# Tile 0's softmax sums on GpSimd in an attention and feed-forward kernel on one core, with the order of all work dealt anew

## The chip, the cores and the metric

One core of a Trainium2 chip (trn2) runs the whole kernel; the other cores are idle. The metric is device time in microseconds for one launch, from the kernel's own start to its end. The kernel before was timed three times: 800.82, 801.04 and 800.82 us.

## The reference

Linear attention whose output goes through one feed-forward block. `q`, `k` and `v` have the shape (8, 8, 576, 64): 8 batches, 8 heads, 576 positions, 64 features.

```python
def _attn_ref(q, k, v):
   q_s = q - np.max(q, axis=-1, keepdims=True)
   q_s = np.exp(q_s)
   q_s = q_s / (np.sum(q_s, axis=-1, keepdims=True) + 1e-09)
   k_s = k - np.max(k, axis=2, keepdims=True)
   k_s = np.exp(k_s)
   k_s = k_s / (np.sum(k_s, axis=2, keepdims=True) + 1e-09)
   kv = np.einsum('bhsd,bhse->bhde', k_s, v)
   return np.einsum('bhsd,bhde->bhse', q_s, kv).astype(np.float32)

def _moe_ref(x, w_in, w_out):        # x: 4608 x 512, w_in: 512 x 2048, w_out: 2048 x 512
    h = x @ w_in
    g = np.maximum(h, 0.0) + np.log1p(np.exp(-np.abs(h)))   # softplus
    return (g @ w_out).astype(np.float32)
```

Between the two, the heads are put side by side: x is 4608 tokens by 512.

## The kernel before, in words

The 4608 tokens are nine tiles of 512 (`TOK`). Tile 0 is worked alone; tiles 1 to 8 are worked in four pairs, whose two matrix products are done by seven block products instead of eight. Float32 products are made of rounded halves (`fp32r`, a high and a low part, three matmuls); only in tile 0 a few products use whole float32 (slower, but no split is needed first): the x of tile 0 (`x_first`) and the first two of its 16 blocks of the hidden layer.

All engines take their work in the order of one long list, `ORDER`, of some 2200 tokens. Each token calls one small function, which issues one to a few instructions on the engine that the function names. There is no scheduler at run time: an engine takes its own instructions strictly in the order of the list, and waits at one whose input is not ready. A second list, `HOMES`, says which slot of on-chip memory each buffer takes; a load into a slot waits until its last reader is done.

Tokens that matter here (tile 0, batch 0):

- `b0`, `b1`: load the two halves of tile 0's q (0.5 MB each). `n`: load the next k and v block (`kv_load`: two small fills of unused rows, the main load from SyncE, the tail's load from ScalarE's queue for the first four). `l3`: load the raw weights of block 3.
- `q0.0`, `q0.1` (`top`): maxima of the two halves of q. `q0.2` (`join`): joins maxima between the two partition groups that share a token's head; four ScalarE copies (`swapped`) and one VectorE maximum. `q0.3`, `q0.4` (`shift`): subtract the maxima; `q0.5`, `q0.6` (`power`): exp on ScalarE; `q0.7`, `q0.8` (`total`): sums of exp, a reduction on VectorE; `q0.12`, `q0.13` (`swap`): a TensorE matmul that joins the sums; `q0.9` (`invert`): their reciprocals; `q0.10`, `q0.11` (`divide`). A trailing `.1` on a q token puts it on GpSimd: before, these are `q0.4.1` and `q0.11.1`.
- `k0.h.i`, for the heads' pair h = 0 to 3: `.1` transposes of k on TensorE, `.2` (`across`) its maxima, `.3` their spread on TensorE, `.4` the subtraction, `.5` exp on ScalarE, `.6` the kv products on TensorE, `.7` (`scale`) reciprocals, `.8` (`keep`) two ScalarE copies of the scaled kv.
- `x0.h.0` (`flip`) a VectorE transpose of q, `.1` its product with kv, `.2` (`take`) out of PSUM, `.3` and `.4` the high and low part of x.
- Weights of block j: `Tj`, `Mj`, `Sj`, `Jj` rebuild float32 words, `Pj` and `Qj` split them in two. ScalarE does T, M and P, VectorE J and Q, a few S and Q are on GpSimd.
- `B0` to `B3`: the first hidden block by whole float32, one matmul per head pair. `Uj`: hidden block j, `Aj`: its softplus on ScalarE, `Gj`: the split of the result, `Oj`: its product with the output weights. `U1` and `O0`, `O1` are whole float32 too.
- `wA.n`: n warm-up matmuls on the identity, whose results nobody reads. They stand where TensorE would be idle before the first products.

At the start `first`, one float per partition, is filled and added to itself on GpSimd (line 1073), before anything else is asked of that engine. Its result is read by nobody.

The list before begins as follows, and the head that matters ends at `U2`:

```
    w0.20 b0 b1 q0.0 n k0.0.1 n q0.1 n n q0.2 q0.3 q0.4.1 l0 q0.5 l1 k0.0.2 k0.1.1 l2 k0.1.2 k0.0.3 k0.2.1 k0.0.4
    k0.0.5 q0.6 k0.1.3 k0.2.2 w5.5 k0.2.3 k0.1.4 k0.2.4 k0.1.5 l3 q0.7 k0.3.1 k0.3.2 k0.0.6 k0.0.7 T0 M0.1 T1 k0.1.6
    q0.8 k0.3.3 q0.12 w1.6 q0.13 k0.2.5 k0.2.6 k0.3.4 k0.3.5 k0.3.6 n z0 M1.1 k0.0.8 q0.9 q0.10 w2.3 k0.1.7 w3.2
```

Of the kernel before, what the change touches and what calls it, by code (L numbers as in the profile page):

```python
# [7 lines left out]
F32 = mybir.dt.float32  # L8
F32R = mybir.dt.float32r
U8 = mybir.dt.uint8  # L10
# [49 lines left out]
    Q9 D9 k1.3.5 q1.8 k1.2.6 k1.2.7 q1.5 q1.7 k1.3.6 k1.3.7 P11 A8 U9 k1.2.8 k1.2.9 D8 q1.9 Q11 q1.10 U10 q1.11 T12 G8  # L60
    D2 D1 x1.0.0 W0 A9 T13 G9 A10 M13.1 U11 M14.1 x1.0.1 O8 M12.1 J13 O9 x1.0.2 k2.0.0 P0 x1.0.3 D11 J12 G10 k1.3.8
    k1.3.9 P12 x1.1.0 Q12 Q0 M15.1 O10 x1.1.1 x1.1.2 T14 U12 P13 Q13 J14 D12 A11 x1.0.4 x1.0.5 x1.1.3 x1.1.4 U13
    x1.2.0 G11 O11 x1.1.5 k2.1.0 k2.1.1 x1.2.1 x1.2.2 x1.2.3 D10 P14 Q14 k2.1.2 A12 T15 J15 x1.2.4 k2.1.3 k2.1.4
    x1.3.0 U14 D0 A13 G12 D4 G13 P15 x1.3.1 A14 O12 x1.2.5 k2.0.1 x1.3.2 x1.3.3 k2.0.2 Q15.1 k2.0.3 k2.1.5 L2 k2.0.4
    O13 k2.0.5 x1.3.4 x1.3.5 U15 G14 k2.0.6 k2.1.6 y1.8 y1.9 y0.11 y1.11 D3 O14 A15 y0.8 G15 O15 q2.0 q2.1 n q2.2
    k2.0.7 k2.0.8 k2.1.7 k2.1.8 U16 U17 k2.0.9 A16 U18 n q2.4.1 q2.6 k2.1.9 k2.2.0 k2.3.0 k2.3.1 A17 U19 q2.3 D15 y0.9
    y1.10 y1.0 A18 y1.1 q2.8 y1.2 D14 k2.2.1 y0.10 D13 L3 y1.3 U20 k2.2.2 k2.3.2 k2.3.3 q2.5 q2.7 k2.2.3 q2.9 k2.2.4
    A19 q2.10 U21 A20 U22 y1.4 R0.0 y1.5 y1.6 A21 U23 x2.0.0 x2.0.1 q2.11 x2.0.2 y2.10 k2.3.4 A22 x2.0.3 k2.2.5 U24
    x2.0.4 y1.7 y0.0 y0.1 x2.0.5 k2.3.5 k2.2.6 A23 q3.0 y2.8 k2.2.7 k2.2.8 k2.2.9 L4 A24 k2.3.6 k2.3.7 y3.8 k2.3.8 U25
    x2.2.0 n n q3.1 k2.3.9 x2.1.0 A25 R0.1 x2.1.1 y2.9 U26 A26 q3.12 U27 A27 y2.11 R4.1.1 x2.1.2 x2.1.3 x2.1.4 U28  # L70
    y0.2 R0.2 x2.2.1 R4.3.1 k3.0.0 U29 q3.2 R4.0.1 y3.10 y3.9 A28 y0.3 y0.4 k3.0.4 y3.11 q3.4 x2.2.2 A29 U30 y0.5
    k3.0.5 q3.6 x2.1.5 x2.3.0 q3.3 x2.2.3 x2.3.1 x2.3.2 x2.2.4 y2.0 x2.2.5 U31 x2.3.3 A30 y2.1 y2.2 x2.3.4 x2.3.5 y2.3
    y0.7 y0.6 k3.1.0 r0.1 e0.0.0.0 A31 F0.2 F0.1 R0.3 U32 A32 F0.0 U33 q4.0 q4.1 q3.5 k3.1.4 q3.7 U34 k3.1.5 k3.1.6
    k3.0.6 A33 U35 q3.8 q3.13 q3.9 A34 q3.10 q4.12 q4.2 k3.0.7 k3.1.7 n U36 y3.0 A35 k3.0.8 y3.1 U37 y3.2 R0.4 y3.3
# [1155 lines left out]
```

## Time and profile before

| what | us |
| --- | --- |
| median of three timed runs | 800.82 |
| the profiled execution, its own time | 800.14 |
| its span, first to last instruction | 798.4 |
| TensorE (PE) busy in the span | 789.0 |
| VectorE (DVE) busy | 643.8 |
| ScalarE (ACT) busy | 516.6 |
| GpSimd (POOL) busy | 130.3 |

The span is the time from the first instruction to the last in one profiled launch; 1.74 us of that launch lie outside it. Its own time is 0.68 us under the median of the timed runs. Busy times are unions of an engine's instructions. A matmul's end is modelled, so "busy" on PE means that the engine had a matmul under way, not that it ran at its peak. In the rows below a start is counted from the span's beginning.

### The profile page before, as it was taken

The numbers are of one execution on the slowest core, as the hardware profiler recorded it, in microseconds if no ns is written. First come the engines' busy times: TensorE is split into PE (matmuls) and PEld (weight loads), VectorE is DVE, ScalarE is ACT, GpSimd is POOL, SyncE is SP. The second block draws the span as 40 slices with busy tenths as digits, with TensorE's granted clock in tenths as the row PEclk, the third lists the DMA queues.
The fourth block names the chain that finished last, engine by engine and source line by source line (L and its number), as shares of the span: only waits on it lengthen the run. The fifth ranks groups of instructions, "written<-read, shape, count | busy, mean of one in ns | idle before, by whom it ended". The sixth has DMA issues, their size and how long they took to land.

```text
span 798.4 us, 11786 instructions
## 1 busy us (share of the span) xinstructions
PE 789.0 (99%) x4196; PEld 646.8 (81%) x4196; DVE 643.8 (81%) x869; ACT 516.6 (65%) x768; POOL 130.3 (16%) x249
## 2 busy tenths in 40 slices
...
GB/s 336 371 344 292 321 252 286 289 295 281 325 276 275 238 276 256 288 292 276 263 322 183 288 281 186 238 219 184 328 136 242 269 145 204 136 215 348 145 51 69
DMA packets 137402, 200.01 MB, mean 251 GB/s; under 512 B 9920, under 2 KB 106432, under 8 KB 132224
## 3 DMA queue, kind: packets, MB, share of 16 engines
...
q14 instruction: 25, 0.20, 0.1%
...
## 4 chain that ended last, share of the span: by engine, by line
PE 94%; DVE 2%; DMA 2%; POOL 1%; ACT 1%; issue 0%; POOLq 0%; SPq 0%; ACTq 0%; DVEq 0%
PE po L980 9%; PE po L981 9%; PE po L982 9%; PE po L872 6%; PE po L874 6%; PE po L873 6%; PE ph L752 5%; PE ph L754 5%; PE ph L753 5%; PE ph L980 4%; PE ph L981 4%; PE ph L982 4%; PE ph L872 3%; PE ph L874 3%; PE ph L873 3%; PE att L544 2%
## 5 line engine op out<-in xcount | busy, mean ns | idle before, releaser
L1026 POOL DMA_DIRECT2D out<-w x108 | 69.7, 652 | 139.9 <-DVE w L1018 136.1
L960 ACT CAST w<-w 128x1024 fp32r<-128x1024 f32 x53 | 55.6, 1052 | 35.0 <-PE po L981 26.5
L963 DVE TENSOR_TENSOR w<-w,w 128x1024 fp32r<-128x1024 f32 x53 | 64.4, 1219 | 12.1 <-ACT w L960 12.0
L980 PE MATMUL po<-w,w 128*128 128x512 f32 x160 | 62.8, 392 | 0.0
L981 PE MATMUL po<-w,w 128*128 128x512 f32 x160 | 62.3, 390 | 0.0
L982 PE MATMUL po<-w,w 128*128 128x512 f32 x160 | 62.3, 389 | 0.0
L944 DVE TENSOR_TENSOR w<-w,w 128x1024 f32<-128x1024 f32 x44 | 53.3, 1215 | 0.3
...
L960 ACT CAST gg<-w 128x1024 fp32r<-128x1024 f32 x33 | 34.7, 1051 | 17.8 <-PE po L981 10.6
L873 PE MATMUL po<-w,w 128*128 128x512 f32 x118 | 46.0, 390 | 0.0
L872 PE MATMUL po<-w,w 128*128 128x512 f32 x108 | 42.6, 394 | 0.0
L874 PE MATMUL po<-w,w 128*128 128x512 f32 x108 | 42.1, 389 | 0.0
L963 DVE TENSOR_TENSOR gg<-w,gg 128x1024 fp32r<-128x1024 f32 x33 | 40.1, 1216 | 1.7 <-ACT gg L960 1.7
L493 DVE TENSOR_REDUCE mx<-kvt 128x128 f32<-128x640 f32 x28 | 36.8, 1317 | 0.3 <-DMA kvt<-in_kv_tail 0.2
L893 DVE TENSOR_TENSOR w<-po,w 128x512 f32<-128x512 f32 x20 | 13.7, 686 | 27.4 <-PE po L874 22.4
L982 PEld LDWEIGHTS po<-w,w 128*128 128x128 f32 x160 | 30.0, 188 | 6.5
L981 PEld LDWEIGHTS po<-w,w 128*128 128x128 f32 x160 | 30.1, 188 | 6.0
L980 PEld LDWEIGHTS po<-w,w 128*128 128x128 f32 x160 | 30.1, 188 | 6.0
L752 PE MATMUL ph<-w,w 128*128 128x512 f32 x88 | 34.8, 396 | 0.0
L753 PE MATMUL ph<-w,w 128*128 128x512 f32 x88 | 34.3, 390 | 0.0
L754 PE MATMUL ph<-w,w 128*128 128x512 f32 x88 | 34.3, 389 | 0.0
L873 PE MATMUL ph<-w,w 128*128 128x512 f32 x82 | 31.9, 390 | 0.0
...
## 6 DMA issues: line engine op xcount, KB each, us to landing
...
```

Source lines behind the costliest of these rows:

```text
L752: nc.tensor.matmul(ph, lhsT=w_hi, rhs=x_hi, start=h == 0, stop=False)
L753: nc.tensor.matmul(ph, lhsT=w_lo, rhs=x_hi, start=False, stop=False)
L754: nc.tensor.matmul(ph, lhsT=w_hi, rhs=x_lo, start=False, stop=h == HP - 1)
L872: nc.tensor.matmul(ph, lhsT=w_hi, rhs=x_hi, start=c == 0 and i in (0, 4), stop=False, **more)
L873: nc.tensor.matmul(ph, lhsT=w_lo, rhs=x_hi, start=False, stop=False, **more)
L874: nc.tensor.matmul(ph, lhsT=w_hi, rhs=x_lo, start=False, stop=c == 1, **more)
L960: nc.scalar.copy(ring[p, i, s, "two"][0], right_of(p, i, s))
L963: engine.tensor_tensor(out=lo, in0=right_of(p, i, s), in1=hi.bitcast(F32), op=ALU.subtract)
L980: nc.tensor.matmul(bank, lhsT=w_hi, rhs=hi, start=begin, stop=False, **more)
L981: nc.tensor.matmul(bank, lhsT=w_lo, rhs=hi, start=False, stop=False, **more)
L982: nc.tensor.matmul(bank, lhsT=w_hi, rhs=lo, start=False, stop=s == NS - 1, **more)
L1026: nc.gpsimd.dma_start(out=rows(n, c)[:, 32 * a:32 * a + 32].rearrange("(b r) e -> r b e", r=32), in_=flipped(n)[32 * a:32 * a + 32, c].rea ...
```

## The change

Six edits, all in one diff:

1. `total` can run on GpSimd. There it is a tree of five additions instead of a reduction: the 32 numbers of each row are added by halves (16 sums, then 8, 4, 2, 1). The scratch space is `qT`, which is not yet in use. Tile 0 uses it for both halves (`q0.7.1`, `q0.8.1`).
2. Tile 0's `join` is done for each half of q by itself (`q0.2` and the new `q0.14`): four copies of 32x32 and one maximum of 128x32 each.
3. `q0.4`, the second subtraction, moves from GpSimd to VectorE.
4. The fills of the first four k and v blocks move from VectorE to GpSimd; all four `n` now stand before the first q token.
5. The addition of `first` to itself gets a token, `g`, and stands behind these four `n`.
6. `ORDER` and `HOMES` are dealt anew, from the first token to the last. 26 warm-up units stand in it instead of 38. Every other token is there as often as before.

The diff, cut to its code and the first lines of the list:

```diff
 ORDER = """
-    w0.20 b0 b1 q0.0 n k0.0.1 n q0.1 n n q0.2 q0.3 q0.4.1 l0 q0.5 l1 k0.0.2 k0.1.1 l2 k0.1.2 k0.0.3 k0.2.1 k0.0.4
-    k0.0.5 q0.6 k0.1.3 k0.2.2 w5.5 k0.2.3 k0.1.4 k0.2.4 k0.1.5 l3 q0.7 k0.3.1 k0.3.2 k0.0.6 k0.0.7 T0 M0.1 T1 k0.1.6
-    q0.8 k0.3.3 q0.12 w1.6 q0.13 k0.2.5 k0.2.6 k0.3.4 k0.3.5 k0.3.6 n z0 M1.1 k0.0.8 q0.9 q0.10 w2.3 k0.1.7 w3.2
-    k0.2.7 k0.1.8 k0.2.8 x0.0.0 w4.2 x0.0.1 T2 x0.1.0 x0.1.1 x0.0.2 k0.3.7 k0.3.8 q0.11.1 x0.2.0 z1 x0.3.0 x0.1.2
-    x0.2.1 x0.2.2 l4 J0 x0.3.1 k1.0.0 B0 B1 M2.1 n J1 T3 M3 x0.3.2 k1.0.1 k1.0.2 J2 S3.1 T4 M4.1 B2 B3 l5.6.7.8.9 L1
-    k1.0.3 k1.0.4 U0 k1.0.5 k1.1.0 A0 x0.3.3 P2 x0.1.3 J4 x0.0.3 x0.2.3 J3 P3 Q2 M5 x0.0.4 x0.1.4 x0.2.4 x0.3.4 Q3 W1
...
+    w0.16 b0 b1 n n n n g q0.0 q0.1 q0.2 q0.3 q0.14 q0.4 q0.5 q0.6 l0 w5.3 k0.0.1 q0.7.1 q0.8.1 l1 k0.1.1 k0.0.2 w1.3
+    k0.1.2 k0.0.3 k0.0.4 k0.0.5 k0.1.3 k0.1.4 k0.2.1 k0.1.5 k0.3.1 k0.0.6 k0.2.2 k0.2.3 k0.3.2 l2 n T0 k0.0.7 M0.1
+    k0.3.3 k0.2.4 k0.2.5 k0.3.4 w2.2 k0.3.5 q0.12 q0.13 k0.1.6 T1 k0.0.8 q0.9 q0.10 l3 q0.11.1 k0.1.7 x0.0.0 k0.1.8 l4
+    k0.2.6 k0.2.7 k0.2.8 k0.3.6 k0.3.7 k0.3.8 n x0.0.1 w3.1 x0.1.0 x0.1.1 T2 x0.2.0 w4.1 J0 x0.3.0 x0.2.1 x0.0.2
+    x0.1.2 B0 k1.0.0 x0.0.3 x0.3.1 M1.1 B1 k1.0.1 x0.2.2 x0.0.4 M2.1 T3 M3 S3.1 B2 x0.3.2 J1 B3 M4.1 U0 k1.0.2 L1
+    k1.0.3 J2 k1.0.4 k1.0.5 k1.1.0 A0 U1 A1 z0 P2 l5.6.7.8.9 J3 x0.2.3 k1.0.6 Q2 k1.1.1 O0 D2 x0.1.3 x0.1.4 x0.3.3 P3
...
+        def join_half(g):
+            if "m" not in state:
+                state["m"] = sm.tile([P, TOK // 8], F32, name="other")
+            gs = slice(g * n, (g + 1) * n)
+            for a in range(4):
+                z = a ^ 1
+                nc.scalar.copy(state["m"][32 * a:32 * a + 32, gs], m[32 * z:32 * z + 32, gs])
+            nc.vector.tensor_tensor(out=m[:, gs], in0=m[:, gs], in1=state["m"][:, gs], op=ALU.max)
...
-        def total(g):
-            nc.vector.tensor_reduce(out=s[:, g * n:(g + 1) * n], in_=half[g], op=ALU.add, axis=AX.X)
+        def total(g, engine=nc.vector):
+            if engine is nc.vector:
+                engine.tensor_reduce(out=s[:, g * n:(g + 1) * n], in_=half[g], op=ALU.add, axis=AX.X)
+                return
+            a, r = half[g], 16
+            tree = qT[:, 2 * g:2 * g + 2].rearrange("p h n -> p (h n)")
+            while r:
+                first = 2 * TOK - 2 * n * r
+                out = tree[:, first:first + n * r].rearrange("p (i r) -> p i r", r=r) if r > 1 else (
+                    s[:, g * n:(g + 1) * n].unsqueeze(2))
+                engine.tensor_tensor(out=out, in0=a[:, :, 0:r], in1=a[:, :, r:2 * r], op=ALU.add)
+                a, r = out, r // 2
...
-        nc.gpsimd.tensor_tensor(out=first, in0=first, in1=first, op=ALU.add)
...
+            elif kind == "g":
+                nc.gpsimd.tensor_tensor(out=first, in0=first, in1=first, op=ALU.add)
...
-                place = dict(engine=nc.vector, queue=nc.scalar) if ahead[0] < HP else {}
+                place = dict(queue=nc.scalar) if ahead[0] < HP else {}
```

## Rows read from the trace of the kernel before

**Rows 1.** The page's first part: busy us, share of the span, instructions, by engine.

```profile
PE 789.0 (99%) x4196; PEld 646.8 (81%) x4196; DVE 643.8 (81%) x869; ACT 516.6 (65%) x768; POOL 130.3 (16%) x249
```

**Rows 2.** Waits of PE, whole run: who waited for whom, us, times, longest.

```profile
PE ph L872 <- ACT ph L882: 0.7, 1, 0.7
```

**Rows 3.** Busy by stretch: length; PE, PEld, DVE, ACT, POOL; clock; DMA share; GB/s.

```profile
10.63:36.47 25.84, 25.63 (x310) 18.35 (x310) 23.88 (x43) 22.12 (x31) 9.39 (x18) 1.00 1.05 379
60.00:100.00 40.00, 40.00 (x231) 32.79 (x230) 39.16 (x57) 39.11 (x50) 1.41 (x9) 1.00 0.86 306
230.00:400.00 170.00, 169.26 (x900) 140.07 (x899) 159.81 (x200) 111.93 (x169) 21.95 (x50) 1.00 0.88 274
```

**Rows 4.** PE in order of time: start us, us, line, operation, tiles, shape, count.

```profile
17.76 0.70 PE L539 MATMUL att<-one,kvt 128*64 128x1 f32 x20
18.32 0.78 PE L544 MATMUL po<-kvt 128*64 128x64 f32 x20
...
28.57 1.88 PE L740 MATMUL ph<-x,w 128*128 128x512 f32 x4
...
32.23 3.60 PE L740 MATMUL ph<-x,w 128*128 128x512 f32 x8
...
36.52 1.17 PE L795 MATMUL po<-w,g 128*128 128x512 f32 x2
```

**Rows 5.** DVE in order of time, the head.

```profile
6.20 0.17 DVE L467 MEMSET kvt<- 64x128 f32 x1
...
6.82 1.22 DVE L610 TENSOR_REDUCE m<-qt 128x32 f32<-128x1024 f32 x1
...
9.37 1.23 DVE L624 TENSOR_TENSOR qt<-qt,m 128x1024 f32<-128x1024 f32 x1
10.51 0.22 DVE L517 TENSOR_REDUCE m<-ph 128x1 f32<-128x64 f32 x1
...
11.64 0.22 DVE L517 TENSOR_REDUCE m<-ph 128x1 f32<-128x64 f32 x1
...
12.99 0.81 DVE L528 TENSOR_TENSOR kvt<-kvt,po 128x640 f32<-128x640 f32 x1
...
18.83 1.20 DVE L630 TENSOR_REDUCE s<-qt 128x32 f32<-128x1024 f32 x1
...
21.10 0.22 DVE L655 TENSOR_SCALAR s<-ph 128x64 f32<-128x64 f32 x1 [0.34 <-PE ph L637]
```

**Rows 6.** ACT in order of time, the head.

```profile
8.07 1.00 ACT L597 COPY other<-m 32x64 f32<-32x64 f32 x4 [6.04 <-DVE m L610]
10.63 1.06 ACT L627 ACTIVATE qt<-qt 128x1024 f32<-128x1024 f32 x1 [1.55 <-DVE qt L624]
...
24.84 1.16 ACT L334 ACTIVATE w<-w 128x1024 uint32<-128x1024 uint8 x1
...
35.87 0.60 ACT L766 ACTIVATE g<-ph 128x512 f32<-128x512 f32 x1
...
38.92 0.62 ACT L724 CAST spare<-x 128x512 fp32r<-128x512 f32 x1
```

**Rows 7.** POOL in order of time, the head.

```profile
10.20 0.44 POOL L1073 TENSOR_TENSOR first<-first 128x1 f32<-128x1 f32 x1 [9.35 <-PE ph L507]
10.61 1.91 POOL L624 TENSOR_TENSOR qt<-qt,m 128x1024 f32<-128x1024 f32 x1
...
22.05 2.88 POOL L659 TENSOR_TENSOR qt<-qt,s 128x1024 f32<-128x1024 f32 x1 [2.83 <-DVE s L656]
```

**Rows 8.** POOL by line and form: count, busy us, mean ns, idle before.

```profile
L369 POOL TENSOR_TENSOR w<-w,w 128x1024 fp32r<-128x1024 f32 x1 | 2.5, 2476 | 6.0 <-ACT w L367 6.0
```

**Rows 9.** Line 1177, tile 0's two loads of q: issue to landing.

```profile
DMA to landing us min/median/max: 4.1/4.7/5.4
```

**Rows 10.** The chain that ended last, in order of time: start us, us, what.

```profile
371.24 4.38 DMA kvt<-in_kv
...
792.74 1.28 POOL out L1026 x2
```

More of the change, by code (lines that the diff above doesn't have):

```diff
@@ L60 @@
[L60 to L74, printed above, removed]
@@ new lines @@
+    X1.1.T1 X1.1.T3 d0.5.7 e0.6.4.0 e0.6.4.1 d0.6.0 o0.c11.0 X1.1.hB22 d0.6.1 X1.1.lB22 X1.1.T2 X1.1.lB21 o0.flip.0.0
+    X1.1.T4 e0.6.6.0 e0.6.6.1 n n X1.0.T3 o0.store.0.0 X1.0.hT3 X1.1.hT2 o0.flip.0.1 X1.0.T2 X1.0.T4 d0.6.2 d0.6.3
+    d0.6.4 d0.6.5 R1.1 Y0.5 d0.6.6 X1.1.lT2 Y0.7 d0.6.7 X1.0.hT1 C1.0.0 X1.0.hT2 X1.0.lT2 X1.0.lT1 o0.c21.1 o0.c21.0
+    o0.c12.0 o0.flip.2.0 C1.0.7 C1.0.1 Y0.6 C1.0.8 C1.0.2 o0.c12.1 X1.1.hT1 R3.2.1 X1.1.hT4 X1.1.lT1 C1.0.3 R1.2
+    o0.store.0.1 X1.1.hT3 X1.1.lT3 C1.1.0 X1.0.lT3 C1.0.4 Y1.8 X1.0.hT4 X1.0.lT4 C1.0.10 C1.0.11 o0.flip.2.1
@@ new lines @@
+    o0.store.2.1 Y1.0 C1.0.5 X1.1.lT4 Y1.1 Y1.2 o0.store.2.0 C1.1.7 Y1.3 C1.1.1 C1.0.6 C1.1.2 C1.1.8 C1.1.3 C1.0.9
+    C1.2.0 Y1.4 C1.0.14 C1.2.7 Y1.5 C1.1.4 k5.0.0 C1.1.10 C1.1.11 C1.1.5 C1.1.9 e1.0.0.0 k5.1.0 k5.0.4 k5.1.4 C1.2.1
+    C1.1.6 C1.0.15 C1.2.2 Y2.8 Y2.0 Y2.1 C1.2.8 R3.3.1 C1.2.3 Y2.2 R1.3 C1.0.12 C1.3.0 C1.2.4 Y2.3 k5.1.5 k5.0.5
+    k5.1.6 k5.0.6 C1.2.10 C1.2.5 R3.4.1 C1.1.14 Y1.7 C1.3.7 C1.3.1 C1.2.11 C1.2.6 C1.1.15 Y2.4 t1.1.0 Y2.5 C1.3.2
+    C1.2.9 C1.3.8 Y3.8 Y3.0 Y3.1 C1.3.3 Y1.6 C1.3.9 C1.4.0 C1.2.14 Y3.2 Y3.3 C1.4.7 R3.5.1 C1.3.4 k5.0.7 C1.3.10
```

288 lines of the change are left out of this document (147 added, 141 removed).

## The prediction

> **What bounds the kernel now.** I read the page's first part first: PE has a matmul under way in 789.0 of 798.4 us [rows 1]. A modelled busy time could hide waits, so the view of PE's waits came next: between its first real matmul and the last stage it waited once, 0.7 us for a ScalarE copy at the start of a pair [rows 2]. PE in order of time then shows where the unbroken stream begins: at 28.57 with `B0` [rows 4]. From there on the run is a fixed amount of matmul work. The change adds and takes away none behind `B0` (each U, O, C, d, k, x token is there as often as before; only `x0.3.1`, 0.86 us, now stands behind `B0` instead of before it). So the time can move in three ways only: the stream begins earlier or later, it gets or loses gaps, or the few us behind the last matmul change. The fourth thing to read is who feeds the stream: in late tile 0 DVE is busy 39.16 and ACT 39.11 of 40 us, and in the first pair's stages DVE 159.81 of 170 [rows 3]. A stream that begins earlier must be fed earlier by engines with almost no idle time.
>
> **Part by part: the head.** I walk the queues in the new order with the old durations.
>
> *Maxima and subtraction (edits 2 and 3).* Before, `join` waited for the four copies of both maxima, 8.07 to 9.07, and the subtraction began at 9.37 [rows 5, 6]. Now the first half's copies run while VectorE takes the second half's maximum. That one can't start before its load has landed, 1.2 + 5.4 = 6.6 us [rows 9], so 6.7 instead of 6.82, and ends at 7.9; the half join is priced as the old one at most, 0.25; the first subtraction begins at 8.15, 1.2 us earlier, and its exp at 10.63 - 1.2 = 9.4 [rows 6]. The second subtraction, 1.91 on GpSimd [rows 7], becomes 1.23 on DVE [rows 5], 9.5 to 10.7. The four additional copies lie in ScalarE's idle time before 9.4 (6.04 us before [rows 6]); without that cover they would cost 1.0.
>
> *VectorE afterwards.* Gone are both sums, 2 x 1.20, and eight fills of 0.17; added is one subtraction, 1.23 [rows 5]: about 2.3 us less. From 10.7 it owes four across steps of 1.13 (10.51 to 11.64), four subtractions of 0.81 and one scale of 0.3 [rows 5]: 10.7 + 4.5 + 3.2 + 0.3 = 18.7, and I add 0.2 for waits on PE's spreads: 18.9. Only then does `invert` come, which began at 21.10 before.
>
> *The trees (edit 1).* No row shows GpSimd adding by halves, so I bound a tree. It adds 512 + 256 + 128 + 64 + 32 = 992 numbers per partition in five instructions. Lower end: 992/1024 of the 1.91 us subtraction, nothing more for the small steps: 1.85. Upper end: 992/1024 of the 2.476 us subtraction of two full operands [rows 8], and for each of five steps the 0.44 us of the one-element addition [rows 7]: 4.6. I take 3.0: the full-operand row is the nearest in kind (2.4), and 0.44 includes the tail of what that addition had waited for.
>
> *Where the trees start (edits 4 and 5).* The one-element addition follows nothing, yet GpSimd was idle 9.35 us before it and it ran at 10.20 [rows 7]; the row names a PE matmul, which it does not depend on, so I read it as the price of the engine's first addition. Eight fills now stand before it. At 0.17 each [rows 5] it moves by 1.4, to 11.6, and ends at 12.0; if that price does not move with it, at 10.64. The first exp is done by 10.5, so the trees run from 12.0 to 18.0. The DVE instructions beside them read k and a maximum in PSUM, unlike the multiplication at 22.05, where GpSimd needed 2.88 instead of 1.91 beside VectorE's own multiplication [rows 7].
>
> The Trainium skill speaks against this edit: GPSIMD Engine Reference, section 4.1, sends elementwise work and reductions along the free dimension to VectorE, and section 3.1 gives GpSimd about 2.6 cycles an element at 1.2 GHz. An estimate by that figure is 992 x 2.6 / 1.2 = 2.15 us a tree, with no price for the small steps; the trees would end at 16.3 and the sum below would stay as it is, since PE's queue gets there at 18.1 by its own route; by the upper end of the rows it would turn into a loss. The rows agree on the size (1.91 to 2.88 for 1024 numbers).
>
> *PE.* The joins of the sums stand before the kv products of heads 1 to 3. `q0.13` can run at 18.1; by the other route (products, spreads and warm-up ahead of it in PE's queue) PE gets there at about 18.1 too. Three products of 0.56 + 0.6 = 1.2 us [rows 4] follow: kv is whole at 22.0, against 23.4.
>
> *ScalarE decides.* `A0` must be done before `O0`, and before, `A0` ended at 36.47 and `O0` began at 36.52 [rows 4, 6], while its bank had been ready since 32.1 [rows 4]: ScalarE's queue was late, not PE. From the first exp to there ScalarE worked 22.1 of 25.84 us [rows 3]. In the new order `T4` (1.16) stands behind `A0`, and one high part of x (0.62) before it [rows 6]: 21.6. Its idle time stays about 3.7: I count 1.9 behind the second exp until kv 0 is subtracted, the rest in small waits for kv 1 to 3. So `A0` ends at 9.4 + 21.6 + 3.7 = 34.7, 1.8 us earlier. PE alone would be ready for `O0` at about 34.4 (kv whole at 22.0, `B0` at 25.2, `B3` done at 29.7, `U1` 3.6, a kv product): 2.1 earlier.
>
> **The head's gain: 1.8.** If a tree takes 4.6, `q0.13` slips to 21.3, kv to 24.9, and `A0` comes to about 37.2: a loss of 0.7.
>
> **Part by part: the stream (edit 6).** Up to the last product of tile 0 the U and O tokens stand in the same order as before. I added up ScalarE's and VectorE's work (durations as above) ahead of every P, Q, A and G in both lists. From `G5` to `G15` the new list has 0.4 to 4.8 us less VectorE work ahead of each G, and between 3.7 less and 1.2 more on ScalarE. Two operands have clearly more ahead of them, `Q4` by 3.7 and `Q7` by 2.1; VectorE's idle 2 us of the head and its lighter load [rows 3, 5] cover them, and without that cover `U4` would wait about 1.9. So the shift of 1.8 can be fed there. In the pairs' stages VectorE is the tight one at 159.81 of 170, and it is the engine that lost 2.3 us of work. ScalarE gets four more switches between exp and softplus tables (45 instead of 41, counted in the lists); ScalarE is idle in 34% of 230 to 400, so I cost them at nothing; without that cover they are some 5 us. New gaps and lost old ones I set to zero on balance. That is the softest term: bounds -0.7 (the old wait [rows 2] also goes) and +4.4, one transfer of a kv block waited for in full [rows 10].
>
> **Part by part: the end.** The last chain ran over GpSimd's twelve store instructions of 0.64 to 794.02 [rows 10]. In the new list at least one store of four stands before the last matmuls, and SyncE's own last stores limit what that brings: 0 to 0.4, I take 0.2.
>
> **Sum.** 1.8 + 0.2 = 2.0 us. The profiled execution's own 800.14 would become 798.1; it lay 0.68 under the median of 800.82, so the forecast for the median is 798.8.
>
> **The rivals.**
>
> *Eaten in the stream.* The head brings 1.8, but the new deal has gaps of 0.5 to 2 us that the old one did not have: for it, the feeding engines at 98% and 94% of a stretch [rows 3]; against it, the sums above. Time 800.3 (a 1.5 us gap).
>
> *Slow trees.* Each tree takes 4.6 or more, because every step waits for the one before on the same engine. For it: the 0.44 us for one element. Against it: the wide rows. Time 801.5; slower than 0.2% only from 5.1 a tree on.
>
> *A load comes too late, slower than before.* Place: the stages of pairs 1 and 2, where DMA engines are busy 0.88 of the time and the chain of the kernel before already ran over one kv load of 4.38 us [rows 3, 10]. Loads wait in SyncE's queue for a free slot and in order; both were dealt anew, and three kv blocks and about a dozen weight blocks stand directly before their use in the list. Price: up to 4.38 for a block that starts one transfer late; time 800.82 - 2.0 + 4.4 = 803.2. It decides from 3.6 us of such waits on. Against it: the old list has as many of these close pairs, and its stream shows no such gap.
>
> *The change does not do what it says.* If the price of GpSimd's first addition is not moved by the fills, trees end at 16.6 and PE's own queue binds at 18.1: the same time as the forecast, so no case of its own.
>
> **How the numbers follow.** Forecast 0.55, eaten in the stream 0.28, slow trees 0.06, late load 0.11. A difference under 0.2% (1.6 us) is about what a measurement of this kernel can't tell from no change; so faster 0.55, same 0.34, slower 0.11. The forecast's own range is 797.2 (ScalarE not binding, 2.1; the old wait gone, 0.7; end 0.4; 0.4 of smaller old gaps) to 799.2; with the stream and the trees it reaches to 801.6, which leaves out the late load and little else.
>
> **What would show it.** Right: exp at 9.4, `first` added at 11.6, trees of five additions 2 to 4 us long, `invert` near 19, kv whole near 22, `A0` done near 34.7, `O0` right behind, one PE wait of 0.7 in the stream. Wrong: PE idle between 60 and 130 or in a pair's stage; trees over 4.3; `A0` not before 36.

## The result, and the profile after

| | before | after |
|---|---|---|
| median (range) | 800.93 us (800.82 to 801.16) | 808.47 us (808.31 to 810.9) |
| ratio, 95% interval | | 1.0101 [1.0082, 1.012] |
| profiled run: its time, span | 800.14, 798.4 | 808.31, 806.5 |
| mean granted clock | 1.000 | 0.993 |
| start of `O0` (L795, after L815) | 36.52 | 41.12 |
| start of the last matmul | 793.40 | 802.09 |
| from its end to the end of the span | 4.68 | 4.17 |

Slower by 7.5 us, 0.94% by the medians (the ratio in the table is that of the means); the forecast was 798.8, and its range ended at 801.6. The bottom rows cut the loss in three: 41.12 - 36.52 = 4.60 in the head (all that stands before `O0`), (802.09 - 793.40) - 4.60 = 4.09 in the stream of matmuls behind it, and the end is 4.68 - 4.17 = 0.51 shorter. Together 8.18; the two profiled launches differ by 808.31 - 800.14 = 8.17.

First the engines' busy times, which hardly differ from [rows 1], and the waits of PE between its first matmul and the last stage (us in total, times, longest):

```profile
PE 792.8 (98%) x4172; PEld 647.5 (80%) x4172; DVE 648.6 (80%) x861; ACT 522.9 (65%) x776; POOL 137.2 (17%) x266
```

```profile
PE att L540 <- DVE r L553: 2.2, 1, 2.2
PE ph L773 <- DVE w L370: 1.8, 1, 1.8
PE po L525 <- DVE m L522: 1.1, 1, 1.1
PE ph L892 <- ACT ph L902: 0.7, 1, 0.7
```

The last line is the old wait of [rows 2]; the other three are new, and VectorE releases all of them. L540 and L545 are the products of a heads' pair with its keys (`k0.h.6`: the sums of exp(k), then kv), L773 is in `U4`, L525 is a spread of maxima (`k0.h.3`). The wait at L525 is there in e5_both too, which is as fast as the kernel before; the other two are what this document is about. By stretch (length; busy PE, PEld, DVE, ACT, POOL with counts; granted clock; DMA share; GB/s):

```profile
24.50:31.30 6.80, 6.80 (x49) 4.62 (x50) 5.29 (x11) 3.82 (x9) 0.00 (x0) 0.50 1.04 351
62.00:65.50 3.50, 3.50 (x10) 2.73 (x9) 3.44 (x4) 1.69 (x2) 0.00 (x0) 0.51 0.00 0
60.00:100.00 40.00, 38.38 (x213) 31.18 (x214) 36.58 (x54) 35.60 (x50) 1.89 (x10) 0.96 0.64 231
230.00:400.00 170.00, 169.34 (x928) 139.15 (x928) 158.55 (x204) 107.94 (x170) 25.93 (x56) 1.00 0.85 270
```

Behind two of the new waits the granted clock is 0.50: TensorE at its lower level, 1.2 GHz. A PE that is "busy" 6.80 of 6.80 us runs at half the clock there; that is why the busy times of the page show nothing. The last two lines answer [rows 3]: VectorE and ScalarE are less busy there than before, not more.

VectorE in order of time, at the first wait (start us, us, operation), then GpSimd from its first addition on, then PE:

```profile
14.32 1.54 DVE L529 TENSOR_TENSOR kvt<-kvt,po 128x640 f32<-128x640 f32 x2
...
20.40 0.22 DVE L675 TENSOR_SCALAR s<-ph 128x64 f32<-128x64 f32 x1
20.65 0.55 DVE L676 RECIPROCAL s<-s 128x64 f32<-128x64 f32 x1
21.31 2.97 DVE L679 TENSOR_TENSOR qt<-qt,s 128x1024 f32<-128x1024 f32 x1
24.20 0.15 DVE L553 TENSOR_SCALAR r<-att 128x1 f32<-128x1 f32 x1
```

```profile
12.58 0.18 POOL L1200 TENSOR_TENSOR first<-first 128x1 f32<-128x1 f32 x1 [10.38 <-issue]
12.73 1.27 POOL L649 TENSOR_TENSOR w<-qt 128x512 f32<-128x512 f32 x1
14.09 1.62 POOL L649 TENSOR_TENSOR w<-w 128x256 f32<-128x256 f32 x3
...
21.29 1.91 POOL L679 TENSOR_TENSOR qt<-qt,s 128x1024 f32<-128x1024 f32 x1 [1.41 <-DVE s L676]
```

```profile
21.55 0.78 PE L545 MATMUL po<-x 128*64 128x64 f32 x20
24.50 1.24 PE L540 MATMUL att<-one,x 128*64 128x1 f32 x20 [2.17 <-DVE r L553]
25.55 1.35 PE L545 MATMUL po<-x 128*64 128x64 f32 x20
```

Both engines multiply half of tile 0 by the same reciprocals, which end at 21.20. GpSimd starts at 21.29 and needs 1.91, its full speed; VectorE starts 0.02 us later and needs 2.97 instead of 1.23: GpSimd's remaining 1.89 and then 1.08 of its own. Before, VectorE was first, at 21.94, took 1.23, and GpSimd needed 2.88 [rows 7]. So in these rows the two don't share the time; who comes second stands until the other has ended. Behind the standing multiplication in VectorE's queue is `k0.1.7`, the scale (L553) that PE waits for. Then the clock falls, and 20 key products (L545) take 1.35 instead of 0.78.

The second wait has the same cause; GpSimd and VectorE at 58 us, `Q5` and `Q4`:

```profile
58.01 2.47 POOL L370 TENSOR_TENSOR w<-w,w 128x1024 fp32r<-128x1024 f32 x1 [7.48 <-ACT w L368]
```

```profile
56.94 1.23 DVE L357 SCALAR_TENSOR_TENSOR w<-w 128x1024 uint32<-128x1024 uint32 x1 [0.29 <-ACT w L335]
58.09 3.48 DVE L370 TENSOR_TENSOR w<-w,w 128x1024 fp32r<-128x1024 f32 x1
```

GpSimd first by 0.08 us; VectorE's subtraction needs 3.48 instead of 1.22, `U4` waits 1.8, and the clock is at 0.51 once more. In the kernel before no multiplication and no subtraction of VectorE is lengthened by GpSimd (L659 takes 1.20 to 1.23 us, L369 1.16 to 1.23); GpSimd's multiplication is, to 2.88. One VectorE addition of 0.68 us takes 0.89 there, at 166 us, beside a reduction on GpSimd.

The Trainium skill's page SBUF — State Buffer, section "SBUF: two separate sides", states this: VectorE and GpSimd have one pair of ports in common, a VectorE operation with two inputs in SBUF and a GpSimd operation that reads SBUF exclude each other for a whole instruction, and whichever starts first has it. The traces agree with the lock and with the order: 2.97 and 3.48 where GpSimd is first, 2.88 for GpSimd where VectorE is. They agree with the condition too: VectorE's subtractions of a maximum in PSUM keep their 0.81 beside a running tree (1.54 for the two at 14.32, which overlap a little).

### The profile page after: what moved, and what is told of

It is laid out like the page before. It is cut to its first block, busy times and chain, and to the rows that moved or that the text cites. A ratio compares the mean times of both kernels' runs of the same rounds, so it can differ in the third digit from the quotient of the medians.

```text
span 806.5 us, 11792 instructions
## 1 busy us (share of the span) xinstructions
PE 792.8 (98%) x4172; PEld 647.5 (80%) x4172; DVE 648.6 (80%) x861; ACT 522.9 (65%) x776; POOL 137.2 (17%) x266
## 4 chain that ended last, share of the span: by engine, by line
PE 92%; DMA 4%; ACT 1%; DVE 1%; SPq 1%; issue 0%; ACTq 0%; DVEq 0%
PE po L1000 9%; PE po L1002 9%; PE po L1001 9%; PE po L892 6%; PE po L894 6%; PE po L893 6%; PE ph L772 5%; PE ph L773 5%; PE ph L774 5%; PE ph L1000 4%; PE ph L1001 4%; PE ph L1002 4%; PE ph L892 4%; PE ph L893 3%; PE ph L894 3%; PE att L545 2%
## 5 line engine op out<-in xcount | busy, mean ns | idle before, releaser
L980 ACT CAST w<-w 128x1024 fp32r<-128x1024 f32 x33 | 34.5, 1051 | 22.8 <-PE ph L1001 8.3
L983 DVE TENSOR_TENSOR w<-w,w 128x1024 fp32r<-128x1024 f32 x33 | 39.9, 1217 | 8.3 <-ACT w L980 8.1
L497 POOL PARTITION_ALL_REDUCE mx<-mx x20 | 21.6, 1082 | 141.9 <-DVE mx L494 141.1
L1000 PE MATMUL po<-w,w 128*128 128x512 f32 x116 | 45.6, 393 | 0.0
L1001 PE MATMUL po<-w,w 128*128 128x512 f32 x116 | 45.2, 390 | 0.0
L1002 PE MATMUL po<-w,w 128*128 128x512 f32 x116 | 45.2, 390 | 0.0
L964 DVE TENSOR_TENSOR w<-w,w 128x1024 f32<-128x1024 f32 x36 | 43.6, 1217 | 1.5 <-ACT w L786 1.3
L893 PE MATMUL po<-w,w 128*128 128x512 f32 x98 | 38.2, 390 | 0.0
L892 PE MATMUL po<-w,w 128*128 128x512 f32 x88 | 34.7, 394 | 0.0
L894 PE MATMUL po<-w,w 128*128 128x512 f32 x88 | 34.3, 389 | 0.0
L1000 PE MATMUL po<-gg,w 128*128 128x512 f32 x80 | 31.3, 392 | 0.0
L1002 PE MATMUL po<-gg,w 128*128 128x512 f32 x80 | 31.1, 389 | 0.0
L1001 PE MATMUL po<-gg,w 128*128 128x512 f32 x80 | 31.1, 389 | 0.0
L893 PE MATMUL ph<-w,w 128*128 128x512 f32 x78 | 30.4, 390 | 0.0
L772 PE MATMUL ph<-w,w 128*128 128x512 f32 x76 | 30.1, 396 | 0.0
L773 PE MATMUL ph<-w,w 128*128 128x512 f32 x76 | 29.9, 394 | 0.0
L774 PE MATMUL ph<-w,w 128*128 128x512 f32 x76 | 29.8, 393 | 0.0
```

The costliest lines, as they stand in the source:

```text
L772: nc.tensor.matmul(ph, lhsT=w_hi, rhs=x_hi, start=h == 0, stop=False)
L773: nc.tensor.matmul(ph, lhsT=w_lo, rhs=x_hi, start=False, stop=False)
L774: nc.tensor.matmul(ph, lhsT=w_hi, rhs=x_lo, start=False, stop=h == HP - 1)
L892: nc.tensor.matmul(ph, lhsT=w_hi, rhs=x_hi, start=c == 0 and i in (0, 4), stop=False, **more)
L893: nc.tensor.matmul(ph, lhsT=w_lo, rhs=x_hi, start=False, stop=False, **more)
L894: nc.tensor.matmul(ph, lhsT=w_hi, rhs=x_lo, start=False, stop=c == 1, **more)
```

## The experiments

My theory after the traces, the *blocking theory*: twice a VectorE instruction on PE's path starts a moment behind a GpSimd one and stands still; PE idles behind it; the clock falls. Rivals: the new order has too much on ScalarE and VectorE ahead of `A0` and `U4` whatever GpSimd does; the trees are too slow.

For each run below: medians in us, the ratio of its mean to that of the kernel before timed beside it (whose medians were 800.49 to 800.93), and from its one profile the start of PE's first transposes of keys (`k0.0.1`, L508; L507 in the kernel before; the expectations call them the first spread of keys) and of `O0`, the head from the one to the other, the time from `O0` to the last matmul, and tile 0's multiplication on VectorE / on GpSimd. What is worked out below from heads and streams compares one profile of each run.

| kernel | median | ratio [95%] | transposes, `O0` | head | `O0` to last | multiplications |
|---|---|---|---|---|---|---|
| before | 800.9 | 1 | 9.11, 36.52 | 27.41 | 756.88 | 1.23 / 2.88 |
| after | 808.47 | 1.0101 [1.0082, 1.012] | 9.71, 41.12 | 31.41 | 760.97 | 2.97 / 1.91 |
| e1_divide_dve | 803.17 | 1.0031 [1.0019, 1.0042] | 10.27, 37.41 | 27.14 | 759.32 | 1.23 + 1.18 / none |
| e2_scale_first | 803.39 | 1.0040 [1.0025, 1.0055] | 9.18, 37.30 | 28.12 | 759.58 | 2.94 / 1.91 |
| e3_warm | 805.50 | 1.0062 [1.0043, 1.0081] | 10.51, 39.32 | 28.81 | 760.92 | 2.97 / 1.91 |
| e4_q4_first | 803.97 | 1.0039 [1.0024, 1.0054] | 9.72, 41.12 | 31.40 | 757.23 | 2.97 / 1.91 |
| e5_both | 800.97 | 1.0003 [0.9994, 1.0013] | 10.59, 37.71 | 27.12 | 757.29 | 1.23 + 1.18 / none |
| e6_trees_alone | 801.95 | 1.0016 [1.0007, 1.0025] | 9.73, 38.28 | 28.55 | 756.90 | 2.97 / 1.91 |
| e7_totals_dve | 803.47 | 1.0033 [1.0021, 1.0046] | 9.55, 38.57 | 29.02 | 759.43 | 1.22 / 2.95 |
| e9_gp_second | 800.31 | 1.0012 [0.9994, 1.0029] | 10.50, 40.29 | 29.79 | 757.25 | 2.97 / 1.91 |
| e12_less_warm | 802.25 | 1.0025 [1.0011, 1.0039] | 8.41, 38.65 | 30.24 | 757.23 | 1.23 + 1.18 / none |
| e10_turned | 800.22 | 1.0005 [0.9990, 1.0019] | 7.77, 36.07 | 28.30 | 757.33 | 1.21 / 1.91 |
| e11_spread_early | 803.26 | 1.0036 [1.0022, 1.0050] | 8.56, 38.85 | 30.29 | 757.29 | 1.21 / 1.91 |
| e13_warm_kept | 800.66 | 1.0001 [0.9992, 1.0010] | 9.87, 37.26 | 27.39 | 757.28 | 1.20 / 1.92 |

**The first block.** e1_divide_dve takes GpSimd's half of the multiplication away.

```
-    ... q0.9 q0.10 l3 q0.11.1 k0.1.7 x0.0.0 ... T2 x0.2.0
+    ... q0.9 q0.10 l3 k0.1.7 x0.0.0 ... T2 q0.11 x0.2.0
```

> The changed kernel with the second half of tile 0's multiplication (q0.11) on VectorE, right ahead of x0.2.0, and not on GpSimd. Blocking theory (a VectorE instruction that starts behind a GpSimd one on the same two-operand work stands still until that one ends, PE idles behind it, and the clock falls): the first multiplication takes 1.23 us instead of 2.97, the wait of 2.2 us at L540 and the stretch of granted clock 0.5 from 24.5 on are gone, A0 ends at 36 to 37.5 instead of 40.1, the U4 wait stays; about 804 (803 to 805.5). New-order theory (ScalarE and VectorE simply have too much ahead of A0 in the new list): one more VectorE instruction of 1.23 makes it no better; A0 at 39 or later, 807 to 810.

803.17, 5.3 us less than the change, though VectorE has one instruction more. VectorE, in order of time, behind the reciprocal, and PE's waits:

```profile
21.87 1.23 DVE L679 TENSOR_TENSOR qt<-qt,s 128x1024 f32<-128x1024 f32 x1
```

```profile
PE ph L773 <- DVE w L370: 1.8, 1, 1.8
PE att L540 <- DVE r L553: 0.4, 1, 0.4
```

The wait of 2.2 is 0.4, and the head is 4.27 shorter. In the stream `U4` still waits 1.8, but the clock stays at 1.00 behind it here; that is 760.97 - 759.32 = 1.65 of the gain, and this edit does not explain it. The new-order theory falls: it had 807 or more.

e2_scale_first leaves the block and moves only the scale that stood behind it.

```
-    ... q0.9 q0.10 l3 q0.11.1 k0.1.7 ...
+    ... q0.9 k0.1.7 q0.10 l3 q0.11.1 ...
```

> The changed kernel with k0.1.7, the scale for which PE waits, ahead of the blocked multiplication and not behind it; the block itself stays (2.6 to 3 us). If the loss runs over the scale: PE's wait of 2.2 us at L540 goes, kv is whole near 24.5, about 805. If it runs over the multiplied half as well: PE waits instead 0.9 to 1.5 us for x0's low part at L735, as it did in e6_trees_alone, and 805.5 to 807.

The multiplication still takes 2.94, and yet the time is 803.39. PE's waits:

```profile
PE ph L773 <- DVE w L370: 1.8, 1, 1.8
PE po L735 <- DVE r L553: 1.3, 1, 1.3
```

Both halves of the expectation come true: the wait at L540 goes, one of 1.3 comes at L735 (`x0.0.1`, the product that makes x) behind the multiplied half, whose transpose ends at 24.50 (the view names the scale that VectorE did after it), and the time is still lower than expected, because the granted clock stays at 1.00 here, in the head and behind `U4`. Of the 5.1 us, 31.41 - 28.12 = 3.29 are in the head, for 0.3 us of work moved past one blocked instruction; 1.39 are in the stream, which the edit does not touch. The price of a block is thus set by what is queued behind it.

e3_warm keeps PE at work in its wait, with 24 matmuls of the identity.

```
-    k0.2.6 k0.2.7 k0.2.8 k0.3.6 k0.3.7
+    k0.2.6 k0.2.7 k0.2.8 w9.12 k0.3.6 k0.3.7
```

> The changed kernel with twelve more warm-up units on PE ahead of k0.3.6, where PE waits 2.2 us for the scale that stands behind the slowed multiplication. If the fall of the clock is a cost of its own: the multiplication still takes 2.9 to 3.0 us, but the granted clock stays 1.0 from 24.5 to 31.3, the kv products and x products of that stretch take 0.43 and 0.7 instead of 0.85 and 1.24, A0 comes about 2 us earlier, and the time is about 806 (805.5 to 807). If PE's rate there is covered by other engines: within 0.5 of 808.3 although the clock is full.

PE in order of time, and the stretch that had a clock of 0.50:

```profile
23.05 2.94 PE L1193 MATMUL ph<-ident 128*128 128x128 f32 x24
26.53 0.78 PE L545 MATMUL po<-x 128*64 128x64 f32 x20
```

```profile
24.50:31.30 6.80, 6.80 (x67) 4.71 (x66) 6.09 (x14) 5.11 (x11) 0.07 (x1) 1.00 1.04 352
```

VectorE's multiplication is as long as in the change, but the clock stays up, and the head is 31.41 - 28.81 = 2.60 us shorter; e1_divide_dve takes 28.81 - 27.14 = 1.67 more away, close to the 2.97 - 1.23 = 1.74 of the block. So of the first loss 1.7 is the block and 2.6 is the clock that fell behind it.

**The second block.** e4_q4_first turns two VectorE tokens round.

```
-    O3 T6 J6 Q4 k1.0.9 U4
+    O3 T6 Q4 J6 k1.0.9 U4
```

> The changed kernel with J6 Q4 dealt as Q4 J6, so that VectorE reaches Q4 (3.48 us in the profile) 0.7 us earlier, ahead of GpSimd's Q5. Blocking theory: Q4 takes 1.2 to 1.3 us, GpSimd's Q5 becomes the longer one, U4's wait of 1.8 us and the stretch of granted clock 0.5 behind 62 go: about 804.7 (1.95 + 1.7 less; 804 to 805.5). Rival, that U4 is late for another operand (P4, or VectorE's backlog as a whole): a wait of over 1 us at L773 stays, 807 or more.

GpSimd and VectorE at the same place:

```profile
58.03 3.24 POOL L370 TENSOR_TENSOR w<-w,w 128x1024 fp32r<-128x1024 f32 x1 [7.47 <-ACT w L368]
```

```profile
56.58 1.22 DVE L370 TENSOR_TENSOR w<-w,w 128x1024 fp32r<-128x1024 f32 x1
57.72 1.22 DVE L357 SCALAR_TENSOR_TENSOR w<-w 128x1024 uint32<-128x1024 uint32 x1
```

Now GpSimd is the one that stands, and nobody waits for it. 803.97, 4.5 less; from `O0` to the last matmul 757.23 instead of 760.97. e1_divide_dve, where `U4` waited too but the clock did not fall behind it, has 759.32: the wait is worth 2.1, the clock 1.65. e5_both, both edits together:

> The two edits of e1_divide_dve and e4_q4_first together. Blocking theory: no VectorE instruction is lengthened in the first 100 us, the granted clock is 1.0 to the end, U4 does not wait. In e1_divide_dve the last matmul began 3.33 us later than in the kernel before, of which 1.95 is U4's wait: about 803.2 - 1.95 = 801.2 (800.8 to 801.7). If a third wait is uncovered: 802 or more.

800.97, no difference from the kernel before. The two blocks, with the clock, are the whole loss, within the interval of 0.1%; the gain that was forecast is not there either.

**Which part of the change did it.** e6_trees_alone gives the kernel before the trees and nothing else; e7_totals_dve takes the trees alone out of the change.

```
-    ... l3 q0.7 k0.3.1 ... q0.8 k0.3.3 ...
+    ... l3 q0.7.1 k0.3.1 ... q0.8.1 k0.3.3 ...
```

> The kernel before, its own order, with one part of the change alone: the two sums of exp(q) as GpSimd trees at their old places in the list. VectorE is rid of 2.4 us, the trees end at about 19.1 by 3.25 each, invert at 19.5 instead of 21.10. Blocking theory: it goes by which multiplication starts first behind invert; VectorE first: 799.5 to 800.9 (GpSimd's takes 2.9); GpSimd first: VectorE's takes 2.9 to 3, PE waits, 803 or more. Rival, the trees themselves are the loss: invert at 21.5 or later and 802 or more with no VectorE instruction lengthened.

> The changed kernel with the two sums of exp(q) back on VectorE at the same places in the list (edit 1 undone, the rest kept). Theory that the trees decide who starts first: the first multiplication then waits for nothing of GpSimd, starts directly behind the reciprocal and takes 1.23 us, GpSimd's takes 2.9; invert comes about 2 us later than in the changed kernel (22.5 to 23); PE waits up to 2 us there. 804 to 807 with U4's wait kept. If GpSimd starts first all the same: VectorE's takes 2.97, and 808 to 811.

e6_trees_alone, 801.95; GpSimd and VectorE behind its reciprocal:

```profile
22.23 1.91 POOL L669 TENSOR_TENSOR qt<-qt,s 128x1024 f32<-128x1024 f32 x1 [1.90 <-DVE s L666]
```

```profile
21.59 0.55 DVE L666 RECIPROCAL s<-s 128x64 f32<-128x64 f32 x1
22.25 2.97 DVE L669 TENSOR_TENSOR qt<-qt,s 128x1024 f32<-128x1024 f32 x1
```

GpSimd is first, PE waits 0.9 at x0's low part, and the clock does not fall. The expectation had 803 for that order; the rival's mark, a loss with no VectorE instruction lengthened, is not there. But `invert` did not come at 19.5, as expected; it came at 21.33, where it had come at 21.10 before (0.4 earlier if both are counted from the first transposes). VectorE, with the sums taken off it, waited for PE instead:

```profile
19.63 0.82 DVE L528 TENSOR_TENSOR x<-x,po 128x640 f32<-128x640 f32 x1 [1.42 <-PE po L524]
21.33 0.22 DVE L665 TENSOR_SCALAR s<-ph 128x64 f32<-128x64 f32 x1 [0.89 <-PE ph L647]
```

Between the two joins of the sums (L647 at 19.43 and 20.99) PE has twelve warm-up matmuls in its queue, as in the kernel before. The trees freed VectorE, but `invert` hung on PE.

e7_totals_dve, 803.47: VectorE first, 1.22, and GpSimd stands; a fall of the clock (0.50 from 24.2 to 27.6, behind waits of 1.0, 0.9 and 0.4) and `U4`'s wait are left. `invert` came at 21.30, 1.2 before what was expected: the sums, 2.42 us, lie in part where VectorE waited 0.90 and 0.73 for PE in the change. So the trees turn the order of the two starts, in either surrounding. How, the line of the multiplication shows; first e7_totals_dve, then the changed kernel (line, engine, operation, count: duration ns min/median/max, first and last start; DVEq and POOLq are the sequencers):

```profile
L679 DVE TENSOR_TENSOR qt<-qt,s x5: 1212/1218/1224, 22.1 to 159.7; 128x1024 f32<-128x1024 f32 x5
L679 POOLq EVENT_SEMAPHORE  x1: 17/17/17, 20.0 to 20.0; - x1
L679 POOL TENSOR_TENSOR qt<-qt,s x1: 2951/2951/2951, 22.2 to 22.2; 128x1024 f32<-128x1024 f32 x1
```

```profile
L679 DVE TENSOR_TENSOR qt<-qt,s x5: 1212/1216/2971, 21.3 to 163.8; 128x1024 f32<-128x1024 f32 x5
L679 DVEq EVENT_SEMAPHORE  x1: 21/21/21, 21.2 to 21.2; - x1
L679 POOL TENSOR_TENSOR qt<-qt,s x1: 1914/1914/1914, 21.3 to 21.3; 128x1024 f32<-128x1024 f32 x1
```

VectorE overwrites the half that GpSimd's first tree has read, so with trees its multiplication has a second wait, an instruction of its own of 21 ns in VectorE's queue, long fulfilled (the tree ended at 16.0). With it VectorE starts 0.10 to 0.11 us behind the reciprocal (21.20 to 21.31; 22.14 to 22.25 in e6_trees_alone), without it 0.03 to 0.04 (21.91 to 21.94 before; 22.10 to 22.14 in e7_totals_dve). GpSimd starts 0.08 to 0.15 behind it in all four. That the second wait is what takes the 0.07 us is read from these rows; no run has it alone. 0.07 us decided 1.7, and with the clock 4.3.

**Turning the order back.** e9_gp_second has the edit of e4_q4_first, and delays GpSimd's multiplication by work that it has to do anyway and three one-element additions.

```
-    ... l3 q0.11.1 k0.1.7 ... A1 z0 P2 ... k1.1.2 z1 k1.1.3 ... J6 Q4
+    ... l3 z0 z1 g g g q0.11.1 k0.1.7 ... A1 P2 ... k1.1.2 k1.1.3 ... Q4 J6
```

> The kernel of e4_q4_first with eight zero fills (z0, z1, which stand later in the list otherwise) and three one-element additions on GpSimd ahead of its multiplication, so that it starts 0.2 us or more behind VectorE's. The work is the same, only the order of the two starts is turned. Blocking theory: VectorE's multiplication takes 1.23 us and GpSimd's 2.5 to 3.0, no wait of 2.2 us, granted clock 1.0 throughout; O0 at 37 instead of 41.1; 803.97 - 4.1 = 799.9 (799.2 to 801.0). Rival, that both engines share the work's time whoever starts first: 803 or more. If GpSimd is still first, it says nothing: 804.

Six of its ten runs lie at 799.4 to 800.4 and four at 803.7 to 805.4. The profiled one is of the upper group, and in it GpSimd starts at 22.08, VectorE at 22.10: the delay was too short there. That the lower group is VectorE first fits, but no trace of it was taken.

Why too short: in the profiles of the new order with its 19 warm-up units the reciprocal ended at 20.68 to 22.09, though exp and trees lay almost alike. PE in order of time, the change, then e5_both:

```profile
3.32 6.46 PE L1193 MATMUL ph<-ident 128*128 128x128 f32 x38 [3.32 <-DVE ident L283]
9.71 0.33 PE L508 MATMUL ph<-ident,kvt 64*64 64x64 f32 x4
```

```profile
3.32 7.34 PE L1193 MATMUL ph<-ident 128*128 128x128 f32 x38 [3.32 <-DVE ident L283]
10.59 0.33 PE L508 MATMUL ph<-ident,kvt 64*64 64x64 f32 x4
```

The same 38 warm-up matmuls last until 9.78 or 10.66, as the granted clock rises to 1.0 at 7.45 us in the one and at 9.28 in the other (a warm-up matmul takes 0.42 us before that and 0.28 behind it), while the first block of keys has landed at 8.7 and 8.9. The reciprocal ends 11.50 after the start of the transposes in both (9.71 to 21.21, 10.59 to 22.09). In the kernel before they began at 9.11. e12_less_warm is e5_both with fewer units. e10_turned has these fewer units too, GpSimd's multiplication kept but delayed, `k0.1.7` ahead of VectorE's and `Q4` ahead of `J6`; e11_spread_early is e10_turned with the transposes of k2 moved up, in the place of the three warm-up units (`w1.3`) there:

```
-    w0.16 b0 b1 ...
+    w0.10 b0 b1 ...
```

```
-    ... q0.9 q0.10 l3 q0.11.1 k0.1.7 ...
+    ... q0.9 k0.1.7 q0.10 l3 z0 z1 g q0.11.1 ...
```

```
-    k0.0.2 w1.3 k0.1.2 ... k0.1.4 k0.2.1 k0.1.5
+    k0.0.2 k0.2.1 k0.1.2 ... k0.1.4 k0.1.5
```

> e5_both with 13 warm-up units ahead of the first spread of keys instead of 19. In the new order the reciprocal behind invert ended 11.5 us after the start of that spread in five profiles out of five, and that start (9.2 to 10.6) followed the end of the warm-up units, later the later the granted clock rose to 1.0, though the block of keys had landed by 8.7 to 9.1. Theory: the warm-up units hold PE's queue; the spread begins at 8.9 to 9.3, the reciprocal ends at 20.4 to 20.8 instead of 22.1, O0 at 36.2 to 37, and the time is 0.5 to 1.3 below e5_both's 801.0: 799.7 to 800.5. Rival, that fewer units keep the clock low for longer: granted clock 0.5 beyond 9.5 and 801.5 or more. Rival, that exp or the trees set invert: no change, 800.9.

> The change with what the runs showed put right: GpSimd's multiplication behind eight zero fills and one addition, so that it starts behind VectorE's; k0.1.7 ahead of VectorE's; Q4 ahead of J6; 13 warm-up units. Blocking theory: no VectorE instruction lengthened, GpSimd's multiplication 2 to 3 us, granted clock 1.0 from 9 us on, O0 at 35.5 to 36.3 (before 36.52), all runs in one cluster, where e9_gp_second had two (799.4 to 800.4 and 803.7 to 805.4): 799.2 to 800.2, below the kernel before by 0.5 to 1.3. If GpSimd is still first in some runs: a second cluster above 803.

> e10_turned with the three warm-up units between the spreads of k0 and k1 taken out (VectorE waited 0.7 us for them, since they write the tile that its maximum reads) and the spread of k2 in PE's wait of 1.1 us behind k1's maximum. If VectorE's chain of four blocks of keys sets the head: the reciprocal 0.7 to 1.2 us earlier than in e10_turned, and up to 1 us less: 798.5 to 799.5. If ScalarE's queue up to A0 binds by now, as the prediction had it: the same as e10_turned within 0.3. If PE's idle time lets the clock fall: 801 or more.

The first transposes came at 8.41, 7.77 and 8.56, as meant, and none of the three got all of that time. The reciprocal ended at 20.68, 21.11 and 20.87, no longer 11.5 but 12.3 to 13.3 behind them, because PE now waited for the second tree before it could join the sums: 0.8, 1.3 and 1.7 us. e10_turned:

```profile
PE ph L657 <- POOL s L649: 1.3, 1, 1.3
```

So the rival that the trees set `invert`, which is not so in the change, holds here. e12_less_warm, behind its waits:

```profile
21.20:28.00 6.80, 6.80 (x83) 5.50 (x80) 5.57 (x12) 4.15 (x11) 0.47 (x3) 0.50 1.01 354
```

No multiplication is blocked here; PE waited 1.1 for a maximum and 0.8 for a tree, and then the clock was at 0.50 as well. The units had not only held PE up, it seems, they had also filled it: in e13_warm_kept, which has them back, no run has a mean clock under 0.998. The first rival of its expectation was right in kind (lower clock, 802.25), but the fall came behind the waits at 21, not at the start. e10_turned has the order turned and the earliest `O0`, 36.07; VectorE, then GpSimd, in its profile:

```profile
21.26 1.21 DVE L679 TENSOR_TENSOR qt<-qt,s 128x1024 f32<-128x1024 f32 x1
```

```profile
21.50 1.02 POOL L1200 TENSOR_TENSOR first<-first 128x1 f32<-128x1 f32 x1
22.48 1.91 POOL L679 TENSOR_TENSOR qt<-qt,s 128x1024 f32<-128x1024 f32 x1
```

Even so only six of its twelve runs are at 799.1 to 799.7 with a mean clock of 0.999 or 1.0, the others at 800.8 to 804.6 with 0.994 to 0.997. So block and clock are two things, as e12_less_warm shows, where GpSimd has no multiplication at all and the clock falls. The slower runs of e10_turned were not traced. e11_spread_early, 803.26, has the same fall at 21.5.

e13_warm_kept puts the units back, adds four in PE's wait and five more additions on GpSimd:

```
-    ... k0.0.5 k0.1.3 ... z0 z1 g q0.11.1
+    ... k0.0.5 w8.4 k0.1.3 ... z0 z1 g g g g g g q0.11.1
```

> e10_turned with 19 warm-up units ahead of the first spread, as the change has them, four units more in PE's wait of 1.1 us behind k1's maximum, and five one-element additions more on GpSimd ahead of its multiplication, so that it starts second also where the reciprocal ends late. e10_turned had runs from 799.1 to 799.7 and others up to 804.6 with a lower mean granted clock. Theory: the waits that the 13 units left ahead of 21 us let the clock fall in those; with the units back all runs lie together, at the lower cluster plus up to 0.7 for the later spread: 799.2 to 800.4, under the kernel before by 0.4 to 1.4. Rival, that another cause lets the clock fall: runs above 802 again. If GpSimd starts first: VectorE's multiplication 2.97.

800.66, eleven runs from 799.84 to 801.92, in one group, VectorE first, and but for its first matmul no wait of PE over 0.7; in its profile GpSimd's half came late (24.10 to 26.02). The expected gain isn't there: ratio 1.0001.

## Why the prediction was wrong, step by step

- *exp earlier by 1.2.* Right: 9.15 against the 9.4 forecast, and the second subtraction at 9.25 on VectorE.
- *VectorE through with the keys at 18.7, `invert` at 18.9.* Wrong by 1.5: 20.40. I walked VectorE's queue from 10.7 and put 0.2 for waits on PE. Its waits are in the trace: 0.90, 0.73 and 0.52, together 2.15.

```profile
11.37 0.23 DVE L518 TENSOR_REDUCE m<-ph 128x1 f32<-128x64 f32 x1 [0.90 <-PE ph L508]
13.25 0.23 DVE L518 TENSOR_REDUCE m<-ph 128x1 f32<-128x64 f32 x1 [0.73 <-PE ph L1193]
16.38 0.23 DVE L518 TENSOR_REDUCE m<-ph 128x1 f32<-128x64 f32 x1 [0.52 <-PE ph L508]
```

  The chain of the keys starts at PE's first transposes, and those had not moved forward; they had moved back by 0.6. The 1.2 us at exp therefore had no way to reach `invert`. Without any block the new head is 27.14 (e1_divide_dve) against 27.41, counted from the transposes: 0.27 gained, not 1.8. Counted from the span's beginning nothing is: `O0` stands at 37.41 there, and stood at 36.52. e6_trees_alone says the same of the sums: 2.4 us taken off VectorE became 1.42 and 0.89 of waits on PE.
- *Trees of 3.0, from 12.0 to 18.0.* The size was near, 3.3 each, but they ended 1.3 late (12.73 to 16.02, 15.98 to 19.29). `first` came at 12.58 and not 11.6: the price before GpSimd's first addition moved with the fills, and was 10.38 instead of 9.35. In the change PE came to the joins at 19.32, so they were not late; had VectorE and PE been as early as forecast, the trees would have taken some 1.2 of the 1.8 (19.29 against 18.1); in e10_turned, e11_spread_early and e12_less_warm PE did wait for them.
- *The multiplication.* Here the prediction failed, for 4.3 us. It had the row, 2.88 instead of 1.91 [rows 7], and used it for the trees alone. It took for granted that the two multiplications would go on as before, with GpSimd's the one that stands, and never asked what decides that. The change adds to VectorE's multiplication a dependence on GpSimd's tree; the rule that an added wait is followed to whoever stands behind it would have led to `k0.1.7` and to PE. As a bound this was due: 1.9 more on VectorE, up to 2.2 on PE. No rival had it.
- *ScalarE decides.* Wrong, and by its own rows: PE's stream was unbroken from `B0` on [rows 2, 4], so PE came to `O0` at 36.52 by its own queue, just as `A0` had ended. In the change PE has no wait between 24.50 and `O0` at 41.12 either; `A0` ended at 40.7, since ScalarE waited 1.8 for the scale and then for PE at its lower clock. The other route of the prediction, 12.4 us from the last kv product to `O0`, was near: 25.02 to 37.71 in e5_both. What it had wrong is the time at which kv is whole: 25.0 without a block and 26.9 with it, not 22.0 (its own numbers, 18.1 and three times 1.2, give 21.7).
- *The stream, zero, bounds -0.7 and +4.4.* 4.09, within the bound, by another mechanism. `Q4` was named as the operand with most ahead of it (3.7), with a wait of 1.9 if its cover were gone; `U4` did wait 1.8, but the cover was there: in e4_q4_first it does not wait. The 2.1 were the block, 1.65 the clock, and 0.35 to 0.45 are left in every run of the new order in which `U4` does not wait (0.02 in e6_trees_alone, which has the old order); one more first matmul behind float32 ones would account for 0.4 (0.82 at 44.30 and 53.54, before at 49.09 alone). The late load, the one slower rival, did not happen.
- *The end, 0.2.* 0.51.
- *PE waited once before.* Not quite: the head had a wait of 0.3 us too (L507 at 10.78, for a maximum). No term rests on it.
- *The clock* was in no term. By the differences above 2.6 + 1.65 = 4.25 us of the 8.2 are work at a clock of 0.50. The prediction priced waits of PE by their length.
